# A bias brought to columns by a DMA transpose, and a new order of pieces, in a fused attention and GELU kernel

## The chip, the cores and the metric

One core of a Trainium2 chip. The time is the device time of one execution in microseconds (us); medians of several executions are given. All runs here are single-core, and the granted TensorE clock in every profiled run is 0.999 or 1.0. Names: TensorE (PE) multiplies matrices, VectorE (DVE) and ScalarE (ACT) work on elements, GpSimd (POOL) does small fills and issues some DMAs, SP only issues DMAs. ScalarE issues DMAs too, in the order of its own instructions, between its other work.

## The reference, cut to what matters

```python
x  = A_x                                   # 1 x 2048 x 640, bf16
xn = layernorm(x)
# A: 32 heads of 20, each position attends to itself and 7 earlier ones, 2 apart
q, k, v = xn @ wqkv ;  attn = softmax(q.k * scale) ;  a = (attn . v) @ wo
# B: a feed-forward layer of width 1536
h = gelu(xn @ w1 + b1) ;  b = h @ w2 + b2
return x + a + b
```

The kernel works on four chunks of 512 positions. A chunk's projections (q, k, v), its 12 pieces of `xn @ w1` ("f1"), its logits and its four output blocks are some 50 pieces of work for TensorE, and the pieces of neighbouring chunks are interleaved.

## The kernel before

A small list scheduler inside the kernel puts the pieces in order at build time. It knows each piece's engine, an estimated duration, what it needs and which buffers it holds, and picks by rank. `RANK` holds offsets to the ranks. Piece names: `pj213` is the projection of chunk 2, matrix 1 (k), part 3; `pc213` its evacuation from the accumulator by ScalarE; `f116` and `ge16` the f1 piece 6 of chunk 1 and its GELU; `xs1` the issue of two DMAs by ScalarE; `o003` part 3 of output block 0 of chunk 0.

```python
for name, n in (("acc", 4), ..., ("v", 2), ..., ("ax", 1), ("oT", 1), ("hT", 18), ...):
    pl.pool(name, n)                       # buffers of each kind
...
pl.add(f"pj{n}{which}{to}", PE, 1.08, r, [...], f("pj", n, which, to), [xnT, ps])      # ps: one "acc"
pl.add(f"pc{n}{which}{to}", SE, 0.52, early, [f"pj{n}{which}{to}"], ..., [ps, buf])
...
pl.add(f"xs{n}", SE, 1.2, n - 1000, [f"at{n}"], f("xs", n), [at, ax])                  # ScalarE issues two DMAs
pl.add(f"xd{n}", DQ, 6.0, n - 1000, [f"at{n}"], f("xd", n), [at, ax])                  # SP issues two
...
pl.add(f"f1{n}{ft}", PE, 1.08, base + 10.0 + 1.0 * ft, [...], f("f1", n, ft), [xnT, ps], 22.5)
pl.add(f"ge{n}{ft}", SE, 0.6, base + 0.0, [f"f1{n}{ft}"], f("ge", n, ft), [ps, hTs[ft]], table="gelu")
```

There are four accumulators ("acc", tiles of 128x512 f32 in the memory space PSUM, which the matmuls here write and ScalarE reads), shared by projections and f1 pieces. There are 18 hidden buffers ("hT"), while two chunks would need 24. And `xs` expands the attention weights over the partitions into `ax`, of which there is one: it can be filled for the next chunk only when VectorE has read the last.

The bias b1 arrives as 12 rows and is needed as 12 columns:

```python
def bias1():                               # in the middle of the first chunk's projections
    b1_tp = psA.tile([P, CH], BF16, tag="acc", name="b1_tp")
    nc.tensor.transpose(b1_tp[:, 0:FT], b1_rt[0:FT, :], ident[0:FT, 0:FT])
    nc.vector.tensor_copy(b1T[:], b1_tp[:, 0:FT])

def expand(queue, n, blocks):
    ax = get(("ax", n), lambda: axp.tile([P, BPC, W, P], BF16, tag="ax", name="ax"))
    for j in blocks:
        queue.dma_start(ax[:, j, :, :], tiles["attn", n][j * H : (j + 1) * H, :, :].unsqueeze(1).to_broadcast([H, NQ, W, P]))
def do_xd(n): expand(nc.sync, n, (0, 1))
def do_xs(n): expand(nc.scalar, n, (2, 3))
```

Of the kernel before, what the change touches and what calls it, by code (L numbers as in the profile page):

```python
# [11 lines left out]
ALU = mybir.AluOpType  # L12
AX = mybir.AxisListType
BF16 = mybir.dt.bfloat16
F32 = mybir.dt.float32
PE, VE, SE, DQ = "pe", "ve", "se", "dq"


class Plan:
# [101 lines left out]
S, D, F, H, W, DIL = 2048, 640, 1536, 32, 8, 2  # L121
P = 128
DH = D // H
PAD = (W - 1) * DIL
KT, FT = D // P, F // P
CH = 512
# [6 lines left out]
MW = 16  # L133
LASTB = S // P - 1
# [4 lines left out]


RANK = {
    "ad02": 53.9, "ad11": 29.1, "av2": -13.3, "f11": 8.8, "f12": -3.3, "gc1": 31.2, "ge3": -70.6, "gj1": 9.7,
    "gj2": -47.4, "o01": 8.4, "o02": -60.5, "o10": 1.1, "o11": -5.1, "o23": -111.4, "oc1": 83, "pj11": -38.5,
    "pj21": -36.7, "qk3": -41.5, "st2": 58.4, "st3": 210.8, "xn1": 20.2, "xn2": 19.2,
}


def make_plan(fns, offsets=RANK):

    pl = Plan(offsets)  # L150
# [6 lines left out]
    def f(kind, *a):  # L157
        return lambda: fns[kind](*a)

    def done(n, which):  # L160
        if n:
            return [f"pc{n}{which}{to}" for to in range(KT)]
        return [f"gc{bl}{g}" for bl in range(BPC) for g, parts in enumerate(GROUPS) if which in [p[0] for p in parts]]

    for n in range(NCH):
        base = n * PERIOD
        prev = base - PERIOD
# [2 lines left out]
        hTs = [("hT", n, ft) for ft in range(FT)]  # L170
# [10 lines left out]
        for bl in range(BPC):  # L181
            xn, tp = ("xn", n, bl), ("acc", "tp", n, bl)
# [11 lines left out]
        if n == 0:  # L194
            for bl in range(BPC):
                for g, parts in enumerate(GROUPS):
                    ps, last = ("acc", "g", bl, g), max(p[0] for p in parts)
# [5 lines left out]
        for which, buf in enumerate((q, k, v)):  # L203
            for to in range(KT if n else 0):
                ps = ("acc", "p", n, which, to)
# [44 lines left out]
        for ft in range(FT):  # L250
            ps = ("acc", "h", n, ft)
            pl.add(f"f1{n}{ft}", PE, 1.08, base + 10.0 + 1.0 * ft, [f"tc{n}{bl}" for bl in range(BPC)], f("f1", n, ft), [xnT, ps], 22.5)
            pl.add(f"ge{n}{ft}", SE, 0.6, base + 0.0, [f"f1{n}{ft}"], f("ge", n, ft), [ps, hTs[ft]], table="gelu")

        for bl in range(BPC):
            ob = ("osb", n, bl)
            O = [("O", n, bl)] if n < NCH - 1 or bl % 2 == 0 else [("acc", "lo", n, bl), ("acc", "hi", n, bl)]
            final = n * BPC + bl == LASTB
            last = None
            for pc in range(5):  # L260
                need = [last] if last else [f"ge{n}{ft}" for ft in range(FT)] + [f"xb{n}", "ld"]
                if pc == 4:
                    need.append(f"ot{n}")
                us = (0.65, 0.65, 0.65, 0.65, 1.08)[pc] if final else (0.82, 0.82, 0.82, 0.82, 1.37)[pc]
                last = pl.add(f"o{n}{bl}{pc}", PE, us, base + PERIOD + 8.0 + 8.0 * bl, need, f("o", n, bl, pc, ("lo",) if final else ("lo", "hi")), O + (hTs if pc == 0 else hTs[3 * pc : 3 * pc + 3] if pc < 4 else [oT]))
            if final:
                pl.add("xl", VE, 0.42, base - 40, ["ld"], f("xl"))
                pl.add("oclo", VE, 0.65, base, [last, "xl"], f("oclo"), O + [ob])
                last = pl.add("ohi", PE, 1.05, base + PERIOD + 90, [last], f("ohi"), O)
                pl.add("ochi", VE, 0.25, base, [last], f("ochi"), O + [ob])  # L270
                continue
            pl.add(f"oc{n}{bl}", SE, 0.78, base, [last], f("oc", n, bl), O + [ob])
            pl.add(f"od{n}{bl}", SE, 0.0, base, [f"oc{n}{bl}"], f("od", n, bl), [ob])
# [4 lines left out]
def kernel(  # L278
# [16 lines left out]
    nc = tc.nc  # L295
# [6 lines left out]
    consts = ctx.enter_context(tc.tile_pool(name="consts", bufs=1))  # L302
    wts = ctx.enter_context(tc.tile_pool(name="wts", bufs=1))
    psA = ctx.enter_context(tc.tile_pool(name="psA", bufs=4, space=bass.MemoryType.PSUM))
# [13 lines left out]
    x_sb = wts.tile([P, NCH * BPC, D], BF16, name="x_sb")  # L318
# [1 line left out]
    w1_sb = wts.tile([P, KT, F], BF16, name="w1_sb")  # L320
    w2_sb = wts.tile([P, FT, D], BF16, name="w2_sb")
    wo2 = wts.tile([P, KT, D], BF16, name="wo2")
    b1_rt = consts.tile([P, P], BF16, name="b1_rt")
    b2bc = consts.tile([P, D], BF16, name="b2bc")
    xlast = consts.tile([P, D], BF16, name="xlast")
    wqkv_v = A_wqkv.rearrange("(t p) n -> p t n", p=P)
    b2_bcast = bass.AP(tensor=B_b2.tensor, offset=B_b2.offset, ap=[[0, P], [1, D]])
    nc.sync.dma_start(x_sb[:, 0, :], x_nb[:, 0, :])
# [6 lines left out]
    for n in range(1, NCH):  # L335
        cs = slice(n * BPC, (n + 1) * BPC)
        nc.sync.dma_start(x_sb[:, cs, :], x_nb[:, cs, :])
    nc.sync.dma_start(w1_sb[:], B_w1.rearrange("(t p) n -> p t n", p=P))


# [6 lines left out]
    ident = consts.tile([P, P], BF16, name="ident")  # L347
# [10 lines left out]
    b1T = consts.tile([P, FT], F32, name="b1T")  # L358

    def constants():  # L360

        with nc.allow_low_precision("sums of zeros and a one"):
            nc.vector.tensor_reduce(
                out=head_of[:], in_=ident[:].rearrange("p (h k) -> p h k", k=NQ), axis=AX.X, op=ALU.add
            )

    def bias1():
        b1_tp = psA.tile([P, CH], BF16, tag="acc", name="b1_tp")
        nc.tensor.transpose(b1_tp[:, 0:FT], b1_rt[0:FT, :], ident[0:FT, 0:FT])  # L369
        nc.vector.tensor_copy(b1T[:], b1_tp[:, 0:FT])  # L370

    mv = consts.tile([P, NCH * BPC, nc.vector.BN_AGGR_DIM], F32, name="mv")
    std = consts.tile([P, NCH * BPC], F32, name="std")
# [3 lines left out]
    tiles = {}  # L377

    def get(key, make):
        if key not in tiles:  # L380
            tiles[key] = make()
        return tiles[key]
# [70 lines left out]
        nc.gpsimd.dma_start(dst, b2bc[:].unsqueeze(1).to_broadcast([P, cs.stop - cs.start, D]), accum_op=ALU.add)  # L453

    def do_xl():
        nc.vector.tensor_tensor(out=xlast[:], in0=x_sb[:, LASTB, :], in1=b2bc[:], op=ALU.add)


    def qkv_tile(n, which):
        if which == 0:  # L460
            return get(("q", n), lambda: qkvp.tile([P, KT, CH], BF16, tag="qT", name="qT"))
        tag = "kT" if which == 1 else "vT"
        return get((tag, n), lambda: qkvp.tile([P, KT, PAD + CH], BF16, tag=tag, name=tag))
# [14 lines left out]
            )  # L478

    def do_gj(bl, g):  # L480
        if bl == 0 and g == 3:
            bias1()
        cs = slice(bl * P, (bl + 1) * P)
        ps = psA.tile([P, BPC, P], F32, tag="acc", name="gps")
        tiles["gps", bl, g] = ps
        slots = [(which, to) for which, a, b in GROUPS[g] for to in range(a, b)]
        for i, (which, to) in enumerate(slots):
            for ti in range(KT):
                nc.tensor.matmul(  # L489
                    ps[:, i, :],  # L490
                    lhsT=wqkv_p[which][:, ti, to, :],
                    rhs=tiles["xnT", 0][:, ti, cs],
                    start=(ti == 0),
                    stop=(ti == KT - 1),
                )
# [21 lines left out]
    def do_qk(n, wp, i):  # L517
        prod = get(
            ("qk", n, wp), lambda: prodp.tile([P, 2, KT, CH], BF16, tag="prod", name="prod")
        )  # L520
        off = PAD - DIL * (2 * wp + i)
        nc.vector.tensor_tensor(  # L522
            out=prod[:, i, :, :],
            in0=qkv_tile(n, 0)[:],
            in1=qkv_tile(n, 1)[:, :, off : off + CH],
            op=ALU.mult,
        )

    def do_lg(n, wps):
        L = get(("L", n), lambda: psL.tile([P, W, P], F32, tag="L", name="L"))  # L530
        for wp in wps:
            logits(L, tiles["qk", n, wp], wp)
# [151 lines left out]
    last = (NCH - 1, BPC - 1)  # L684

    def do_oclo():
        osb = outp.tile([P, D], BF16, tag="osb", name="osb")
        tiles["osb", last] = osb
        nc.vector.tensor_tensor(out=osb[:, 0:CH], in0=tiles["lo", *last][:], in1=xlast[:, 0:CH], op=ALU.add)  # L689
        nc.sync.dma_start(out_sd[LASTB * P :, 0:CH], osb[:, 0:CH])  # L690

    def do_ohi():
# [3 lines left out]
    def do_ochi():  # L696
        osb = tiles["osb", last]
        nc.vector.tensor_tensor(  # L698
            out=osb[:, CH:D], in0=tiles["hi", *last][:, 0 : D - CH], in1=xlast[:, CH:D], op=ALU.add
        )  # L700
        nc.scalar.dma_start(out_sd[LASTB * P :, CH:D], osb[:, CH:D])

# [2 lines left out]
    with tc.manual_schedule(engines=engines):  # L705

        idle = psA.tile([P, CH], F32, tag="acc", name="idle")
        for _ in range(WARM):
            nc.tensor.matmul(idle[:, 0:P], lhsT=ident[:], rhs=ident[:], start=True, stop=True)
        for t in make_plan(fns).run():  # L710
            t["fn"]()
# [30 lines left out]
```

## Time and profile before

| | before |
|---|---|
| time, median of 3 runs | 215.1 us (215.06 to 215.31) |
| span of the profiled run | 212.9 us |
| first f1 matmul starts, last matmul ends | 25.48, 210.11 us |
| longest TensorE wait after the first 8 us | 0.2 us |

TensorE carries the kernel, almost without a gap. The prediction below shows the lines for this.

### The profile page before, as it was taken

What the parts mean: (1) busy time and instruction counts of PE and PEld (TensorE: products, weight loads), DVE (VectorE), ACT (ScalarE), POOL (GpSimd) and SP (SyncE); (2) the same over time, 40 slices, a digit from 0 to 9 for tenths busy, and PEclk for the clock granted to TensorE, in tenths of its full rate; (3) what the DMA queues carried; (4) which work ended last, traced back from release to release, by engine and by line L of the source; (5) the groups of instructions that cost most, each with busy time, mean ns of one, the idle gap of its engine ahead of it and who ended that gap; (6) DMA issues with size and microseconds to landing.
All of it is one profiled execution on the core that took longest, in us unless ns stands there. A gap on an engine that the chain in (4) does not pass through costs nothing.

```text
span 212.9 us, 3943 instructions
## 1 busy us (share of the span) xinstructions
PE 206.1 (97%) x1665; PEld 121.2 (57%) x1690; DVE 174.2 (82%) x176; ACT 106.8 (50%) x190; POOL 19.5 (9%) x36
## 2 busy tenths in 40 slices
PE   7899999999999999999999999999999999999994
PEld 7799844654544556556555555554555455555552
DVE  2849999459999999999999999999499789982001
ACT  3567899689565733635428273420297321351210
POOL 2000000000011015101001010110101011101220
PEclk9999999999999999999999999999999999999999
DMA  6999417973939579977002180211021822202223
GB/s 211 364 363 381 78 31 198 386 67 41 228 115 140 76 261 211 197 115 190 0 3 31 17 210 4 31 7 27 2 31 14 216 32 31 26 8 32 34 31 62
DMA packets 23433, 23.95 MB, mean 112 GB/s; under 512 B 9080, under 2 KB 20600, under 8 KB 23416
## 3 DMA queue, kind: packets, MB, share of 16 engines
q1 hardware_dynamic: 17832, 16.49, 28.0%
q0 software_dynamic: 4144, 4.92, 17.3%
q10 hardware_dynamic: 1440, 2.29, 3.7%
q8 instruction: 13, 0.21, 0.4%
q14 instruction: 4, 0.03, 0.0%
HBM read 10.00 MB, written 7.54 MB: 82 GB/s over the span
## 4 chain that ended last, share of the span: by engine, by line
PE 95%; DMA 1%; DVE 1%; issue 1%; ACT 0%
PE lo L668 26%; PE hps L637 24%; PE pps L472 23%; PE gps L489 8%; PE hi L670 8%; PE L L541 4%; DMA x_sb<-in_A_x_dram 1%; PE tp L429 0%; DVE stats L388 0%; DVE stats L389 0%; ACT xnT L433 0%; DVE xn L415 0%; DVE mv L390 0%; DVE osb L698 0%; PE b_tp L369 0%
## 5 line engine op out<-in xcount | busy, mean ns | idle before, releaser
L637 PE MATMUL hps<-xnT,w_sb 128*128 128x512 bf16 x236 | 53.9, 379 | 0.3 <-issue 0.2
L668 PE MATMUL lo<-w_sb,hT 128*128 128x512 bf16 x186 | 52.6, 379 | 0.0
L615 DVE TENSOR_TENSOR pv<-vT,ax 128x2560 bf16<-128x2560 bf16 x32 | 45.9, 1484 | 4.9 <-PE L L541 2.9
L522 DVE TENSOR_TENSOR prod<-qT,kT 128x2560 bf16<-128x2560 bf16 x32 | 45.5, 1484 | 0.0
L670 PE MATMUL hi<-w_sb,hT 128*128 128x128 bf16 x192 | 40.3, 219 | 0.3
L648 ACT ACTIVATE hT<-hps,b1T 128x512 bf16<-128x512 f32 x48 | 31.4, 687 | 17.0 <-PE hps L637 13.7
L637 PEld LDWEIGHTS <-w_sb 128*128 128x128 bf16 x240 | 22.8, 98 | 26.8 <-issue 0.4
L675 ACT CAST osb<-lo 128x512 bf16<-128x512 f32 x15 | 8.8, 585 | 50.9 <-PE hi L670 22.9
L624 DVE TENSOR_TENSOR pv<-pv 128x5120 bf16<-128x5120 bf16 x12 | 33.9, 2822 | 0.3
L668 PEld LDWEIGHTS <-hT 128*128 128x128 bf16 x192 | 18.7, 98 | 22.6 <-issue 0.2
L681 POOL DMA_DIRECT2D out_dram<-osb x15 | 12.9, 862 | 110.4 <-ACT osb L676 110.4
L668 PE MATMUL lo<-wo,oT 128*128 128x512 bf16 x74 | 22.1, 379 | 0.1
L670 PEld LDWEIGHTS <-hT 128*128 128x128 bf16 x192 | 18.4, 98 | 1.9
L670 PE MATMUL hi<-wo,oT 128*128 128x128 bf16 x80 | 16.9, 219 | 0.3
L472 PE MATMUL pps<-xnT,wk_sb 128*128 128x512 bf16 x71 | 16.9, 380 | 0.2
L472 PE MATMUL pps<-xnT,wq_sb 128*128 128x512 bf16 x72 | 16.9, 380 | 0.2
L472 PE MATMUL pps<-xnT,wv_sb 128*128 128x512 bf16 x73 | 16.9, 379 | 0.1
L689 DVE TENSOR_TENSOR osb<-lo,xlast 128x512 bf16<-128x512 f32 x1 | 0.7, 690 | 16.1 <-PE lo L668 16.1
L507 ACT CAST kT<-pps 128x512 bf16<-128x512 f32 x15 | 8.8, 584 | 8.8 <-PE pps L472 8.6
L668 PEld LDWEIGHTS <-oT 128*128 128x128 bf16 x80 | 7.8, 98 | 9.4
L472 PEld LDWEIGHTS <-wk_sb 128*128 128x128 bf16 x75 | 8.6, 118 | 7.5 <-issue 0.4
L472 PEld LDWEIGHTS <-wv_sb 128*128 128x128 bf16 x75 | 8.6, 117 | 7.2
(63 smaller groups left out, 208.2 us busy)
## 6 DMA issues: line engine op xcount, KB each, us to landing
w_sb<-in_B_w_dram SPq DMA_DIRECT2D x2, 1920.0 KB, 11.5
out_dram<-osb POOLq DMA_DIRECT2D x15, 160.0 KB, 3.4
ax<-attn SPq DMA_DIRECT2D x8, 256.0 KB, 5.1
ax<-attn ACTq DMA_DIRECT2D x8, 256.0 KB, 5.5
x_sb<-in_A_x_dram SPq DMA_DIRECT2D x3, 640.0 KB, 11.4
out_dram<-x_sb SPq DMA_DIRECT2D x3, 640.0 KB, 4.7
out_dram<-b2bc POOLq DMA_DIRECT2D x3, 640.0 KB, 7.7
wq_sb<-in_A_wqkv_dram SPq DMA_DIRECT2D x1, 800.0 KB, 4.9
```

The source lines that it names most:

```text
L472: nc.tensor.matmul(ps[:], lhsT=wqkv_p[which][:, ti, to, :], rhs=xnT[:, ti, :], start=(ti == 0), stop=(ti == KT - 1),)
L489: nc.tensor.matmul(ps[:, i, :], lhsT=wqkv_p[which][:, ti, to, :], rhs=tiles["xnT", 0][:, ti, cs], start=(ti == 0), stop=(ti == KT - 1),)
L507: nc.scalar.copy(dest[:, to, off : off + CH], tiles["pps", n, which, to][:])
L522: nc.vector.tensor_tensor(out=prod[:, i, :, :], in0=qkv_tile(n, 0)[:], in1=qkv_tile(n, 1)[:, :, off : off + CH], op=ALU.mult,)
L615: nc.vector.tensor_tensor(out=pv[:, i, :, :].rearrange("p t (j c) -> p t j c", j=BPC), in0=qkv_tile(n, 2)[:, :, off : off + CH].rearrange( ...
L624: nc.vector.tensor_tensor(out=ta[:], in0=ta[:], in1=tb[:], op=ALU.add)
L637: nc.tensor.matmul(ps[:], lhsT=w1_sb[:, ti, ft * P : (ft + 1) * P], rhs=tiles["xnT", n][:, ti, :], start=(ti == 0), stop=(ti == KT - 1),)
L648: nc.scalar.activation(hT[:], tiles["hps", n, ft][:], ACT.Gelu_apprx_tanh, bias=b1T[:, ft : ft + 1], scale=1.0)
L668: nc.tensor.matmul(lo[:], lhsT=lhs, rhs=rhs[:, 0:CH], start=first, stop=last)
L670: nc.tensor.matmul(hi[:, 0 : D - CH], lhsT=lhs, rhs=rhs[:, CH:D], start=first, stop=last)
L675: nc.scalar.copy(osb[:, 0:CH], tiles["lo", n, bl][:])
L681: nc.gpsimd.dma_start(rows, tiles["osb", n, bl][:], accum_op=ALU.add)
```

## The change

Its intent: take the small bias transpose and its accumulator away from TensorE, and use an order of pieces found anew. The core of the diff:

```diff
 RANK = {
-    "ad02": 53.9, "ad11": 29.1, "av2": -13.3, "f11": 8.8, ... "xn1": 20.2, "xn2": 19.2,
+    "ad00": 208.1, "ad12": 95.5, "f11": 58.8, ... "qk1": -408.6, "st1": 163.4, "st3": 223.3, "xn1": -2.5,
 }
+    pl.add("b1", VE, 0.1, -90, [], f("b1"), after=21.0)
-            pl.add(f"ge{n}{ft}", SE, 0.6, base + 0.0, [f"f1{n}{ft}"], ...)
+            pl.add(f"ge{n}{ft}", SE, 0.6, base + 0.0, [f"f1{n}{ft}", "b1"], ...)
-                pl.add("xl", VE, 0.42, base - 40, ["ld"], f("xl"))
+                pl.add("xl", VE, 0.42, base, [f"xn{n}{bl}"], f("xl"))
...
-    b1_rt = consts.tile([P, P], BF16, name="b1_rt")
+    b1_rt = consts.tile([MW, P], BF16, name="b1_rt")
+    b1_t = consts.tile([P, MW], BF16, name="b1_t")
+    nc.gpsimd.memset(b1_rt[:], 0.0)
-    xlast = consts.tile([P, D], BF16, name="xlast")
...
         nc.sync.dma_start(x_sb[:, cs, :], x_nb[:, cs, :])
+    nc.sync.dma_start_transpose(b1_t[:], b1_rt[:])
     nc.sync.dma_start(w1_sb[:], B_w1.rearrange("(t p) n -> p t n", p=P))
...
-    def bias1(): ...                       # the TensorE transpose and its copy
+    def do_b1():
+        nc.vector.tensor_copy(b1T[:], b1_t[:, 0:FT])
```

The residual of the last block is now added in place into `x_sb` and no longer into `xlast`.

## The prediction

> **What bounds the kernel now.** I read the summary of the page first, then what TensorE waited for, then the chain of work that ended last, then the stretches, and last the DMA issues and the first 27 us, where the change sits.
>
> ```profile
> span 212.9 us, 3943 instructions
> PE 206.1 (97%) x1665; PEld 121.2 (57%) x1690; DVE 174.2 (82%) x176; ACT 106.8 (50%) x190; POOL 19.5 (9%) x36
> PE 95%; DMA 1%; DVE 1%; issue 1%; ACT 0%
> ```
>
> TensorE is busy for 97% of the span and carries 95% of the chain. A busy TensorE need not be a full one, so I asked what it waited for. This is the whole answer:
>
> ```profile
> PE idle L709 <- POOL ident masks.py:199: 1.5, 1, 1.5
> PE tp L429 <- DVE xn L415: 0.7, 1, 0.7
> PE gps L489 <- ACT xnT L433: 0.2, 1, 0.2
> PE hps L637 <- issue: 0.2, 1, 0.2
> ```
>
> Nothing after the first 8 us is a wait of any size. The chain gives the rate at which matmuls really follow each other:
>
> ```profile
> 0.74 3.02 DMA x_sb<-in_A_x_dram
> 6.47 0.47 PE tp L429 x5
> ...
> 11.77 0.56 PE gps L489 x10
> 12.33 0.11 PE b_tp L369
> 12.44 0.04 issue
> 12.48 13.00 PE gps L489 x230
> 25.48 0.22 PE hps L637
> ...
> 117.24 2.16 PE hps L637 x10
> ```
>
> From these rows: a 512-column matmul costs 0.216 us (10 in 2.16), a 128-column one of the first chunk 0.0565 (230 in 13.00). In the second output column block it is 0.055 (the pair lo and hi starts every 0.27). The work, counted from the kernel: 240 + 225 + 272 matmuls of 512 columns are 159.2; 272 short ones 15.0; 300 first-chunk projections 17.0; the logits 9.6 (one group of 80 in 2.30, six of 40 in 1.21); 20 transposes 1.1. Together 201.9 us. The chain runs on TensorE from 6.47 to 210.11, which is 203.6 us. So only 1.7 us is not matmul streaming, of which 0.76 is the first transposed block's way through ScalarE (6.94 to 7.70) and 0.15 is the bias transpose (12.33 to 12.48). The front of 6.5 us is the load of x and the first normalisation; the tail of 2.8 us is the last addition and store.
>
> VectorE is the second engine. Its waits late in the kernel show how much room it has:
>
> ```profile
> 152.82 1.49 DVE L615 TENSOR_TENSOR pv<-vT,ax 128x2560 bf16<-128x2560 bf16 x1 [2.90 <-PE L L541]
> 170.93 5.69 DVE L615 TENSOR_TENSOR pv<-vT,ax 128x2560 bf16<-128x2560 bf16 x4 [2.00 <-DMA ax<-attn]
> 191.66 1.49 DVE L630 TENSOR_TENSOR oT<-pv 128x2560 bf16<-128x2560 bf16 x1 [0.85 <-PE hi L670]
> ```
>
> It loses some 6 us there without TensorE ever stopping.
>
> **What the Trainium skill says.**
> - "TensorE: Matmul & The Clock Gate", section "Wait — 56ns, not 53.3ns?": back-to-back warm matmuls start every 55.6 ns at 128 columns and 215.7 ns at 512. The trace agrees (56.5 and 216 ns), so the matmuls here are at their streaming rate and an order of pieces cannot make them shorter.
> - "DMA: Bandwidth & Descriptors", section "DMA Transpose (X-bar)": a DMA transpose is issued from SP or ACT, takes 2-byte types, and wants a partition dimension that is a multiple of 16. That is why the 12 rows of b1 now lie in a zeroed 16-row tile. The twelve transposes of xn in this trace went from SP and landed 2.4 to 11.1 us after issue, median 3.2.
> - Same page, section "Two DMAs through the same engine are not ordered": a DMA that reads what an earlier one wrote needs the earlier one's semaphore, waited for by the issuing engine. So SP will stand still until b1 has landed, and whatever is behind it in SP's order stands too. No run here shows that yet.
>
> **The change part by part.**
> 1. The TensorE transpose of b1 goes, and with it its use of one of the four accumulators. It saves the 0.15 us between 12.33 and 12.48, and on VectorE a cast of 0.17 us that had waited 1.93. A like copy comes back on VectorE, with the DMA transpose as its source, just ahead of the second chunk's rstd. Gain on TensorE: 0.15 us.
> 2. A zeroing of 16x128 on GpSimd comes before the identity. The 128x128 memset took 0.20 there, so about 0.1 to 0.2 us later for the identity; TensorE's warm-up matmuls have 0.7 us between their end and the first real work. Cost: 0.
> 3. The DMA transpose stands on SP between the last x load and the load of w1. The lines that count:
>
> ```profile
> 3.34 1.24 SPq L334 DMA_DIRECT2D b_rt<-in_B_b_dram  x1
> 4.62 4.14 SPq L337 DMA_DIRECT2D x_sb<-in_A_x_dram  x3
> 8.81 1.71 SPq L338 DMA_DIRECT2D w_sb<-in_B_w_dram  x1
> ```
>
> b1 is queued behind the load of wv (issued 2.74, landed 9.1 later, so 11.8) and ahead of the second chunk of x, whose first user starts at 13.7. It lands between: about 12.3. SP then issues the transpose (1.2 us for the 128x640 ones, so at most that) and w1 from about 13, instead of 8.81. But the DMA engines have x until its last part lands (issued near 6.3, at most 11.9 later: about 18), so w1's data would have started around 16 to 17 in either kernel. It landed at 8.81 + 14.3 = 23.1 before; I expect 23.1 to 24.1, and its first reader starts at 25.3. Cost: 0, with 1.2 to 2.2 us of margin. The transpose itself should land by about 19, and its copy stands on VectorE at about 22.
> 4. The last block's residual is added in place into x, not into a tile of its own: the same 0.49 us instruction, moved from before the first softmax into the second half. Cost: 0.
> 5. The order. I walked the new order by hand with the durations above (prod and pv step 1.42, pv additions 2.83, one f1 piece 1.08, one output piece 0.81 or 1.36). The third chunk's x is now normalised before the second's, and VectorE must wait for it (landing about 16.5 to 17 where the second's rows end at 15.7): some 1 us later start of the first products, 25.9 against 24.59. They end at 37.2, and the first logits are due at 25.3 + 12 x 1.08 = 38.3. All twelve f1 pieces of chunk 0 come before the projections of chunk 1; xn of its last block is then ready at about 36.7, its transpose at 39.1 to 40.0, needed at 40.6. VectorE then waits some 2.3 us for the projections (49.7 to 52.0), which the old order did not. The three places where TensorE reads a fresh attention output: chunk 0 needed at 94.9, ready 94.0; chunk 1 needed 129.9, ready 123.8; chunk 2 needed 169.2, ready 168.6. Last one: needed 196, ready 190. So the path stays on TensorE everywhere, with the thinnest margins 0.5 to 0.9 us. Cost: 0, or one or two small stops.
>
> Sum: 215.1 - 0.15 = 214.95 if nothing stops; the most that a perfect order could take away besides is the 0.8 us of unexplained gaps, and each missed margin adds some tenths. I say 215.0.
>
> **The rivals.**
> - *SP's wait becomes the new bound.* If b1 lands late, or the transpose holds up the queue, w1 comes after 25.3 and TensorE stops; f1 is the next piece in both orders, so it could not go round it. For: DMA is saturated until 21 us (363 to 395 GB/s in the stretches) and w1 leaves SP 4 us later. Against: what SP issues late only waits in the rings anyway. It would make 216 to 219.
> - *VectorE becomes the bound.* The new order starts its heavy part 1 us later and gives it another 2.3 us hole; the three margins are below 1 us in two places. For: 19.9 of 20 us busy in the stretches from 60 to 140. Against: it has 6 us of waits after 150 and its last output is due 4 to 6 us after it is ready. Three stops of half a microsecond: 216.5.
> - *The order helps more than the bias.* The gaps of the old order vanish: 214.1. The waits leave no more to win.
>
> **Range and chances.** The floor is 215.1 less 0.15 less the 0.8 of small gaps: 214.1. Above, one rival at a moderate size gives 216.5. Eight in ten: 214.1 to 216.5. Faster by 2% means 4.3 us, and the count of matmuls leaves 1.7 in all: 1%. Slower by 2% needs a stop of over 4 us on TensorE, which only a late w1 or a blocked queue could make: 4%. Within 2%: 95%.
>
> **What would show it.** Right: TensorE still at 96 to 97% busy; no row for the bias in the chain; w1 issued at about 13 and landed before 25; first projection of the second chunk at about 40.6 without a wait. Wrong: a TensorE wait of over 1 us on w1, on VectorE's attention output or on ScalarE's evacuation; the bias copy waiting on VectorE at 22; a second wait of SP behind the transpose that delays the transposes of xn.

## More of the kernel before

One more place of the old kernel's timeline matters in the end. It shows what went on while ScalarE issued the second chunk's expansion (columns: start us, duration us, engine, line, operation, count, and in brackets the idle time before):

```profile
91.61 0.58 ACT L507 CAST vT<-pps 128x512 bf16<-128x512 f32 x1 [0.49 <-PE pps L472]
...
92.89 2.34 ACTq L599 DMA_DIRECT2D ax<-attn  x2
93.58 2.32 PE L472 MATMUL pps<-xnT,wq_sb 128*128 128x512 bf16 x10
...
95.84 1.28 PE L541 MATMUL L<-prod,head_of 128*32 128x256 bf16 x40
95.91 1.09 ACT L507 CAST qT<-pps 128x512 bf16<-128x512 f32 x2
...
97.04 1.27 PE L472 MATMUL pps<-xnT,wq_sb 128*128 128x512 bf16 x4
```

For 2.34 us ScalarE evacuates nothing. TensorE has work all the same: the end of an output block until 93.5, two projection pieces into two free accumulators, and a group of logits at 95.84. None of these waits for ScalarE.

## The result, and the profile after

| | before | after |
|---|---|---|
| time, median of 6 runs each | 215.12 us (215.06 to 216.11) | 216.18 us (216.08 to 216.29) |
| ratio of fast runs | | 1.0041 (95%: 1.0023 to 1.0058) |
| span of the profiled run | 212.9 | 213.9 us |
| first f1 matmul starts | 25.48 | 24.93 |
| last matmul ends | 210.11 | 210.74 |
| between the two | 184.63 | 185.81 |

A ratio here is the mean time of one kernel's fast runs over that of the other's fast runs of the same rounds, so it is not quite the ratio of the medians. By the 2% measure the two are the same; the loss of 0.4% is nevertheless clear of noise.

The last three rows of the table divide the span into three. Before the first f1 piece the new kernel gains 0.55 us. Of this, 0.24 is the first x load, which ended at 3.52 instead of 3.76 in this execution. Between the first f1 and the last matmul it loses 1.18. What follows (last addition and store) is 0.37 longer in this pair of profiles. Sum: -0.55 + 1.18 + 0.37 = 1.0, the difference of the spans.

So the loss lies where both kernels run the same matmuls. TensorE's list of waits in the new kernel (who, for whom, us in total, times, longest) names it at once:

```profile
PE idle L707 <- POOL ident masks.py:199: 1.6, 1, 1.6
PE pps L469 <- ACT kT L502: 1.1, 1, 1.1
PE tp L426 <- DVE xn L412: 0.5, 1, 0.5
PE gps L484 <- ACT xnT L430: 0.2, 1, 0.2
```

The second row was not there before: one stop of 1.1 us, on an evacuation of k by ScalarE. The timeline around it:

```profile
79.95 0.58 ACT L502 CAST kT<-pps 128x512 bf16<-128x512 f32 x1 [0.49 <-PE pps L469]
...
80.83 1.24 PE L469 MATMUL pps<-xnT,wv_sb 128*128 128x512 bf16 x5
80.90 1.21 SPq L597 DMA_DIRECT2D ax<-attn  x2
80.90 2.39 ACTq L597 DMA_DIRECT2D ax<-attn  x2
...
82.67 0.12 PEld L469 LDWEIGHTS <-wv_sb 128*128 128x128 bf16 x1
83.33 0.59 ACT L502 CAST kT<-pps 128x512 bf16<-128x512 f32 x1 [2.80 <-issue]
...
83.97 4.48 PE L469 MATMUL pps<-xnT,wv_sb 128*128 128x512 bf16 x20 [1.09 <-ACT kT L502]
```

ScalarE evacuates at 79.95, and its next evacuation is at 83.33. Between them its queue issues the expansion of chunk 1, from 80.90 (when VectorE had read the old weights for the last time) to 83.29. The "2.80 <-issue" says that it waited for nothing else the profile shows. At 82.67 TensorE has loaded the weights of its next piece and may not write.

But why does one late evacuation stop a kernel with four accumulators? The built program answers: the matmul that stopped (`pj221`) waits for the evacuation of `pj214`, only two projections before it. In this stretch all projections alternate between two accumulators. The other two hold `f116` and `f117`, computed at about 66 us, whose GELUs stand much later in ScalarE's order because no hidden buffer is free for them. The old order had the same two accumulators taken in the same way. It only had its expansion elsewhere. The planner does not see the stop: run on its own, without the chip, it ends TensorE's last piece at 209.24 us with either order, and in its plan of the new one `pc214` is done at 82.26 us and `pj221` starts at 82.48, since it counts 1.2 us for the issue.

This gives theory A: the new order lost 1.1 us because it put ScalarE's issue (2.39 us, which the scheduler takes for 1.2) into a run of projections that has two accumulators. Theory B: SP's wait for b1 and the later load of w1 cost something. Theory C: the new order loses in many small gaps, of which this one is only the most visible.

### The profile page after: what moved, and what is told of

It is laid out like the page before. It is cut to its first block, busy times and chain, and to the rows that moved or that the text cites. A ratio compares the mean times of both kernels' runs of the same rounds, so it can differ in the third digit from the quotient of the medians.

```text
span 213.9 us, 3968 instructions
## 1 busy us (share of the span) xinstructions
PE 207.2 (97%) x1689; PEld 120.9 (57%) x1689; DVE 174.0 (81%) x176; ACT 110.5 (52%) x192; POOL 19.7 (9%) x37
## 4 chain that ended last, share of the span: by engine, by line
PE 89%; DVE 5%; ACT 2%; DMA 1%; ACTq 1%; issue 0%
PE lo L666 26%; PE hps L635 24%; PE pps L469 18%; PE gps L484 8%; PE hi L668 7%; PE L L539 4%; DVE pv L613 2%; DMA x_sb<-in_A_x_dram 1%; ACTq L597 1%; ACT L569 1%; DVE attn L587 1%; ACT e L569 0%; PE tp L426 0%; DVE rs L582 0%; DVE stats L385 0%; DVE stats L386 0%
## 5 line engine op out<-in xcount | busy, mean ns | idle before, releaser
L666 PE MATMUL lo<-w_sb,hT 128*128 128x512 bf16 x192 | 53.6, 379 | 0.0
L666 PE MATMUL lo<-wo,oT 128*128 128x512 bf16 x80 | 23.1, 379 | 0.0
L385 DVE BATCH_NORM_STATS2 stats<-x_sb 128x6 f32<-128x320 bf16 x16 | 7.3, 459 | 8.2 <-DMA x_sb<-in_A_x_dram 8.2
L687 DVE TENSOR_TENSOR osb<-lo,x_sb 128x512 bf16<-128x512 f32 x1 | 0.7, 692 | 16.1 <-PE lo L666 16.1
L450 POOL DMA_DIRECT2D out_dram<-b2bc x4 | 5.3, 1336 | 87.7 <-DMA out_dram<-x_sb 87.7
```

The source lines that it names most:

```text
L666: nc.tensor.matmul(lo[:], lhsT=lhs, rhs=rhs[:, 0:CH], start=first, stop=last)
```

## The experiments

All were correct. The first four ran on one chip beside 11 runs of the kernel before (median 215.33 us), the last three on another beside 11 runs (215.39 us). Each had 5 timed rounds.

**The bias alone, in the old order.** TensorE's pieces stand as before, without the transpose.

```diff
 (the changed kernel)
-RANK = { ...the new offsets... }
+RANK = { ...the old offsets... }
-                pl.add("xl", VE, 0.42, base, [f"xn{n}{bl}"], f("xl"))
+                pl.add("xl", VE, 0.42, base - 40, ["ld"], f("xl"))
```

> The new way of the bias (DMA transpose, 16-row tile, in-place residual) with the old order of pieces; TensorE's order is the old one but for the removed transpose. Theory A (the loss comes from the new order: one stop of 1.09 us at 83 us, where ScalarE issues the expansion of the attention weights while only two accumulators are free): ratio to the kernel before 0.998 to 1.000, 214.7 to 215.1 us, no TensorE wait above 0.3 us after the first 8 us. Theory B (the loss comes from SP waiting for b1 and the later load of w1): about 1.004, 216 us.

Measured: 214.96 us, ratio 0.9976 (0.9956 to 0.9996). Its whole list of TensorE waits:

```profile
PE idle L708 <- POOL ident masks.py:199: 1.6, 1, 1.6
PE gps L485 <- ACT xnT L431: 0.3, 1, 0.3
```

No stop, and a small gain. Theory B falls. SP did wait, and w1 did leave later, as these rows of SP's queue in this run show:

```profile
4.39 3.75 SPq L339 DMA_DIRECT2D x_sb<-in_A_x_dram  x3
11.54 1.20 SPq L340 DMA_TRANSPOSE b_t<-b_rt  x1
12.78 1.21 SPq L341 DMA_DIRECT2D w_sb<-in_B_w_dram  x1
```

w1 was issued at 12.78 (8.81 before), and landed 10.4 us later, at 23.2, against 23.1 before; its first reader starts at 24.92. The wait is real and costs nothing.

**The order alone, with the bias still transposed on TensorE.**

```diff
 (the kernel before)
-RANK = { ...the old offsets... }
+RANK = { ...the new offsets... }
-                pl.add("xl", VE, 0.42, base - 40, ["ld"], f("xl"))
+                pl.add("xl", VE, 0.42, base, [f"xn{n}{bl}"], f("xl"))
```

> The new order with the bias still transposed on TensorE. Theory A: ratio 1.004 to 1.006, 216.1 to 216.4 us, with the same TensorE stop of about 1.1 us near 83 us released by a ScalarE evacuation. Theory B: 1.000, 215.1 us.

Measured: 216.06 us, ratio 1.0027 (1.0004 to 1.0049), a little below the expected range. By medians it is 1.10 us slower than the bias alone of the same rounds. The stop is there, 1.0 us on the evacuation of k. Without the DMA transpose the loss remains, so the order makes it.

**ScalarE's two issues for chunk 1 moved to SP.** Every compute engine keeps its order.

```diff
     def do_xs(n):
-        expand(nc.scalar, n, (2, 3))
+        expand(nc.sync if n == 1 else nc.scalar, n, (2, 3))
```

> The changed kernel with the second chunk's two expansion DMAs of ScalarE issued from SP; every compute engine keeps its order. Theory A: the stop at 83 us goes, ratio 0.998 to 1.000, 214.7 to 215.1 us. Theory C (the new order loses in many small gaps and the stop is only where one of them shows): the stop goes but the time stays above 215.7 us. If the four issues on one queue come late, VectorE would wait for the weights near 94 us and TensorE for the attention output at 96 us.

Measured: 215.35 us, ratio 0.9993 (0.9973 to 1.0013). The ratio lies in the range for A; the time lies 0.25 us above it, and below that for C. The stop at 83 us is gone, and another of half its size has come at 109 us. Of TensorE and ScalarE there:

```profile
108.65 1.07 ACT L502 CAST vT<-pps 128x512 bf16<-128x512 f32 x2 [3.72 <-DVE pv L613]
...
109.29 1.89 PE L469 MATMUL pps<-xnT,wv_sb 128*128 128x512 bf16 x8 [0.49 <-ACT vT L502]
```

ScalarE could not evacuate the first v pieces of chunk 3, since VectorE still read the v buffer of chunk 1 (two exist), and again two accumulators were not enough to wait it out. In the changed kernel the same evacuation waited 2.60 us, but there TensorE was already 1 us late and lost nothing more. The first stop had hidden the second.

**Four accumulators, with ScalarE's hold left in place.** The GELUs of the two early pieces go directly behind them. That needs two more hidden buffers; the space comes from letting the softmax maximum and reciprocal live in the tile of the sums.

```diff
-    hp = ctx.enter_context(tc.tile_pool(name="hp", bufs=18))
+    hp = ctx.enter_context(tc.tile_pool(name="hp", bufs=20))
 ...
-        for t in make_plan(fns).run():
+        order = make_plan(fns).run()
+        early = [t for t in order if t["name"] in ("ge16", "ge17")]
+        order = [t for t in order if t not in early]
+        at = [t["name"] for t in order].index("f117") + 1
+        for t in order[:at] + early + order[at:]:
             t["fn"]()
```

> The changed kernel with the GELUs of the two early f1 pieces of chunk 1 moved forward (two more hidden buffers; the softmax maximum and reciprocal share the tile of the sums to make room), so that all four accumulators rotate during the projections of chunk 2. ScalarE still spends about 2.4 us issuing the expansion at 81 us. If two free accumulators are half of the cause: no stop at 83 us, ratio 0.998 to 1.000, 214.7 to 215.1 us. If ScalarE's absence alone does it, whatever the number of accumulators: stop of about 1 us, 216.2 us.

Measured: 215.08 us, ratio 0.999 (0.9966 to 1.0015). ScalarE is away just as long, and TensorE no longer notices. Of ScalarE's timeline, then TensorE's whole list of waits:

```profile
81.03 2.40 ACTq L597 DMA_DIRECT2D ax<-attn  x2
83.47 0.58 ACT L502 CAST kT<-pps 128x512 bf16<-128x512 f32 x1 [2.80 <-issue]
```

```profile
PE idle L707 <- POOL ident masks.py:199: 1.6, 1, 1.6
PE tp L426 <- DVE xn L412: 0.7, 1, 0.7
PE gps L484 <- ACT xnT L430: 0.2, 1, 0.2
```

The stop at 109 us is absent too, although ScalarE waited there for VectorE longer (3.85 us) than with the issues on SP (3.72). The number of free accumulators is half of the cause. (This run also changed the softmax tiles; the three-accumulator run below does not, and agrees.)

**The changed kernel again**, unaltered, as the reference on the second chip.

> The changed kernel once more, as the reference on this chip for the two beside it. Ratio to the kernel before 1.003 to 1.006, with the TensorE stop of about 1.1 us at 83 us.

Measured: 216.16 us, ratio 1.0041 (1.0026 to 1.0056), the stop 1.1 us. It repeats.

**ScalarE's two issues for chunk 1 moved to GpSimd**, which was idle.

```diff
     def do_xs(n):
-        expand(nc.scalar, n, (2, 3))
+        expand(nc.gpsimd if n == 1 else nc.scalar, n, (2, 3))
```

> The changed kernel with the second chunk's two expansion DMAs of ScalarE issued from GpSimd, which [...]idles at 81 us; SP keeps its two. If ScalarE's hold is the cause: no TensorE stop above 0.3 us near 83 us; ratio 0.998 to 1.000, some 1.1 us below the changed kernel. The SP issue of all four left a second stop of 0.5 us at 109 us, where an evacuation waited for the attention products of VectorE; if that came from the late landing of the weights (SP needed 4.2 us for four issues) it is gone here, else it stays.

Measured: 215.77 us, ratio 1.0016 (1.0002 to 1.003), outside the expected range. The stop at 83 us is gone here as well, and the half microsecond at 109 us stays:

```profile
81.38 1.14 POOL L597 DMA_DIRECT2D ax<-attn  x2 [19.57 <-DVE pv L613]
...
82.91 4.48 PE L469 MATMUL pps<-xnT,wv_sb 128*128 128x512 bf16 x19
```

```profile
PE pps L469 <- ACT vT L502: 0.5, 1, 0.5
```

The first fence shows that GpSimd issued both in about 1.14 us (spans on GpSimd are rough) and that the stopped piece now starts at 82.91. My guess that the second stop came from SP's slow issues (4.20 us for four) is refuted: VectorE's products end at the same time here as there, and the stop is 0.50 against 0.49. It belongs to VectorE's pace and the two accumulators. It explains 0.5 of the 0.65 us by which this run's median lies above the three-accumulator run of the same rounds; the rest I leave open.

**Three accumulators.** Only `ge16` is moved forward (19 hidden buffers).

```diff
-    hp = ctx.enter_context(tc.tile_pool(name="hp", bufs=18))
+    hp = ctx.enter_context(tc.tile_pool(name="hp", bufs=19))
 ...
+        early = [t for t in order if t["name"] == "ge16"]      # placed behind f117, as above
```

> As the four-accumulator run, but only one of the two early f1 pieces has its GELU moved forward, so three accumulators rotate. By the times of the changed kernel's trace (evacuation of the last k piece done at 83.92; the piece that then waits would be due at 83.75 instead of 82.67) the stop is 0.1 to 0.3 us instead of 1.09. Ratio 0.999 to 1.001, about 0.9 us below the changed kernel. If the number of accumulators acts otherwise, say through ScalarE's load, the stop keeps its size.

Measured: 215.12 us, ratio 0.9987 (0.9975 to 0.9999), 1.04 us below the changed kernel of the same rounds by medians. The list of waits has no row for a projection, but the expected small stop is there. The timelines from 81 to 85 us show it, first of this run, then of the run with four accumulators:

```profile
82.80 2.49 PE L469 MATMUL pps<-xnT,wv_sb 128*128 128x512 bf16 x10
```

```profile
82.85 2.32 PE L469 MATMUL pps<-xnT,wv_sb 128*128 128x512 bf16 x10
```

The same ten matmuls take 0.17 us longer here. In the trace one of them, at 84.06, starts 0.389 us after the one before it instead of 0.216, just after ScalarE's late evacuation ended at 84.00. So the stop shrank from 1.09 to 0.17 us, within the 0.1 to 0.3 expected from the number of accumulators alone.

Taken together, with the time from the first f1 matmul to the last matmul read from each profile's chain. This figure leaves the load at the front and the store at the end out. The times come from three sessions, in which the kernel before had medians of 215.12 (the first row and the changed kernel), 215.33 and 215.39 us, so across sessions only the third column compares well:

| run | time us | first f1 to last matmul us | stops of TensorE in it, us |
|---|---|---|---|
| before | 215.12 | 184.63 | none |
| bias alone | 214.96 | 184.73 | none |
| order alone | 216.06 | 185.75 | 1.0 |
| changed | 216.18 | 185.81 | 1.1 |
| changed, again | 216.16 | 185.78 | 1.1 |
| issues on SP | 215.35 | 185.21 | 0.5 |
| issues on GpSimd | 215.77 | 185.27 | 0.5 |
| three accumulators | 215.12 | 184.73 | 0.2 |
| four accumulators | 215.08 | 184.56 | none |

The middle stretch is 184.56 to 184.77 us plus the stop, in every run. This leaves almost no room for theory C. The changed kernel's trace, whose 1689 matmul records are complete, says the same: in this stretch no other step from one matmul to the next is more than 0.1 us over its streaming time. The new order has one fault of 1.1 us and, behind it, one of 0.5. The bias alone in the old order has the lowest ratio, 0.24% below the kernel before, at the edge of what the rounds resolve; they do not separate it from the runs with three and four accumulators (0.9987 and 0.999).

## Why the prediction was right or wrong

The time fell into the range (216.18 against 214.1 to 216.5, 215.0 expected), and "within 2%" was right. But the upper end of the range came from two rivals that did not happen, and the one thing that did was not among them: a gain of 0.15 us was expected, and 1.06 us were lost. That the range held is luck. Of the prediction's own signs, those for "right" all came (TensorE 97% busy, no row for the bias in the chain, w1 issued at 12.92, the first projection of chunk 1 at 40.12 without a wait), and one of those for "wrong" came as well: a TensorE wait of over 1 us on ScalarE's evacuation. So the danger was named, but no term of the sum was worked out for it. The steps:

- *TensorE bounds the kernel, and an order cannot shorten the matmuls.* Right: from the first f1 to the last matmul 184.63 us before, and 185.81 - 1.09 = 184.72 in the new order.
- *The bias transpose costs TensorE 0.15 us.* Right in sign, too small. From the end of the first x load to the first f1 matmul it is 21.72 us before (25.48 - 3.76), 21.41 in the changed kernel (24.93 - 3.52) and 21.48 in the bias alone (24.92 - 3.44): 0.2 to 0.3 us. The last 240 projection matmuls of chunk 0 alone took 13.71 us with the transpose among them (11.77 to 25.48) and 13.40 without.
- *The extra fill on GpSimd costs nothing.* Right: TensorE's first wait, for the identity, is 1.6 instead of 1.5 us.
- *SP's wait is hidden.* Right, and nearly in the figures: w1 issued at 12.92 (about 13 predicted) and landed 10.2 us later at 23.1 (23.1 to 24.1), the transposed bias landed 6.9 us after its issue at 11.68, so at 18.6 (19), its copy on VectorE at 21.69 (22) without a wait.
- *The walk through the new order.* Most places that I walked to came out well: first products 25.32 (25.9), logits 37.81 (38.3), first projection of chunk 1 at 40.12 without a wait (40.6), VectorE's wait for it 2.5 us (2.3), the attention outputs of chunks 0 to 2 ready at 94.37 (94.0), 124.10 (123.8) and 169.53 (168.6), none of them waited for. xn of chunk 1's last block was ready earlier than walked, at 35.10 (36.7).
- *"So the path stays on TensorE everywhere, with the thinnest margins 0.5 to 0.9 us. Cost: 0, or one or two small stops."* This is the step that failed. The walk followed VectorE to the end, but the last ScalarE time that it names is 36.7 us, and after that it took every evacuation as done in time. It left out that ScalarE issues DMAs in its own order (2.39 us at 80.90), and that two of the four accumulators were held. The term was 0; it measured 1.09 us.
- *The rivals.* None of the three came about: SP's wait stayed hidden, the order cost time where the third had it save some, and after the first 8 us TensorE waited for no result of VectorE in the changed kernel. VectorE's margins did matter, but through the v buffer and only once the first stop was removed.

## What to carry to other kernels

When checking an order of pieces, follow the engine that empties the accumulators through every instruction in its queue, DMA issues included, and ask at each how many accumulators are really free just then, not how many exist. A piece computed early whose consumer has no buffer to write to takes an accumulator out of the rotation for as long as it waits; finding it a buffer can be worth more than shortening the hold. And look again after removing a stop, since a later and smaller one may have been hidden behind it.

## What the Trainium skill lacked or had wrong

- "DMA: Bandwidth & Descriptors", section "Issuing engines are not separate DMA queues", calls the sequencer's time to initiate a DMA "usually small relative to the DMA itself". Here ScalarE's two issues held it for 2.39 us, with the transfers landing 4.0 to 7.4 us after issue, and with two accumulators held that stopped TensorE for 1.09 us. No page says what it costs when the issuing engine is also the one that evacuates accumulators.
- "Perfetto Trace Analysis", section "DMA Instruction — HWDGE (DVE, Sync)", describes one descriptor generator, which the issuing sequencer locks while it uses it, and gives no size for this. The lock alone does not explain the times here. At 80.90 us SP and ScalarE issued two each: the first of each took 0.57 and 0.58 us side by side, SP's second 0.59, and only ScalarE's second was long, 1.77. For chunk 0 it was SP's second that was long (1.73, of 2.47 for the pair), and for chunk 2, at 134.75, the pairs took only 1.21 and 1.48. The four issues on SP, with none of ScalarE beside them, took 0.58, 0.59, 1.18 and 1.70, together 4.20. What makes an issue long stays open.
- "TensorE: Matmul & The Clock Gate", section "Back-to-back issue gap", gives about 81 ns per matmul of 128 columns and about 131 ns at 512 for streams of weight load and matmul. Here every matmul has its own weight load and the chain shows 56 ns (240 in 13.40 us) and 216 ns (10 in 2.16 us), the figures that the same page gives for a single gap.
- "DMA: Bandwidth & Descriptors", section "DMA Transpose (X-bar)", has no duration for a small transpose. One of 16x128 took 1.19 us to issue on SP, about as long as one of 128x640 (1.20), and landed 6.9 us after its issue behind loads still in flight.
